# Where the negative maxima and the first of four sums stand on VectorE, and the order of the first sections, in a fused attention and GEGLU kernel

## The chip, the cores and the metric

The kernel runs on one core of a Trainium2 chip. Its metric is the device time of one execution in microseconds (us). Before the change the median of three runs is 2544.25 us (2543.74 to 2545.1).

A core has a TensorE (PE, matrix products; its weight loads, PEld, overlap the products), VectorE (DVE), ScalarE (ACT), GpSimd (POOL) and SyncE (SP, which here issues the transfers). The engines work side by side and wait for one another through semaphores.

## The reference

All is fp32: 2048 tokens of 576 numbers, 32 heads of 18, a hidden width of 4608.

```python
xn = layernorm(x)
qkv = xn @ wqkv                               # 576 x 1728
scores = einsum("bhqd,bhkd->bhqk", q, k) * 18 ** -0.5
s = (softmax(scores) @ v) @ wo
g = silu((gelu(xn @ w_gate) * (xn @ w_up)) @ w_down)   # 576 x 4608, twice; 4608 x 576
out = x + s * g
```

## The kernel before

**Arithmetic.** Products whose operands must be exact are made from fp32 numbers cut into a high and a low part (fp32r, `split`): high by high, high by low, low by high. Most matrix products use 64 rows of the array, so that two run side by side, one on the upper and one on the lower 64 rows ("row halves"). Only the products that add up attention's values (`acc`, L782) take all rows.

**Sections.** After the layer norm and the projections the feed-forward part is cut into 144 sections, 4 blocks of 512 tokens by 36 sections of 128 hidden units. A section's PE work begins with 27 pairs of matmuls (L413), pg for gate and pu for up. Then comes gelu on ACT and DVE: a square, DVE's first product L427, with pu the copy and product L438, the tanh L443, the last product L446 ("gelu's end"), and the cut of the hidden values (`finish`). Two sections together (G = 2) give the hidden values of one run of products with w_down.

**Sums with w_down.** `half_downs` (from L482) multiplies the hidden values with w_down. It is called one section later. Each sum is a bank py of 128 × 288, made of products on both row halves (L473); when the last one is in, `add_down` (L454) adds it into Y on DVE (L461). In most sections the run has eight sums, with banks taken in the order "mmsmfmss" and every second section; in sections 2 to 11 it has four ("smss"). The letters are the three groups of PSUM banks: "f" (two banks, shared with pg and pu), "m" (three, shared with the maxima and acc) and "s" (three, shared with the scores).

`half_downs` also calls what is left of gelu (`FF["rest"]`) from between its products: PE passes a mark, a tiny ACT copy waits on it, and tanh comes behind that copy. In the last run of a token block (`late = 2`) this happens one sum later than elsewhere, and L446 then follows the first sum added.

**Attention between the sections.** Sections 10 to 137 carry attention as specials spread between their gate and up pairs: a unit is 4 heads by 512 queries and takes 4 sections. A score pe (L747) is followed by its exponential on ACT (L748). The maximum over keys is needed one unit ahead: 40 places earlier a product pm (L709) is made and DVE reduces it (L712). When a unit's maxima are complete, `max_neg` (L719 to 728) forms the negative maxima on DVE: a reduction nm (L724), a copy to fp32r (L725), the subtraction that gives the low part (L726) and a transpose (L727), and sends them to DRAM (L728). `max_rows` then loads them as extra rows of the queries q. This happens in every fourth section: 12, 16, ... 132. There `max_neg` stands ahead of gelu on DVE. A reciprocal (L816) follows in the same section after the eight sums.

**The first sections.** Sections 0 to 9 hold no scores; `FIRST` says how many pairs of maxima for the first unit each holds. The first unit's `max_neg` stands in section 8. Ahead of section 0 SP issues the first keys KS and queries q; the first raw tile of w_down is loaded (`load_down`, L540) when section 1 is issued.

**Order.** PE's order is the program's. For the other engines a scheduler sets the order; `kept` and `keep_in_program_order` hold an instruction to the program's order, and `no_sync(a, b)` puts a behind b on their engine without a semaphore.

Of the kernel before, what the change touches and what calls it, by code (L numbers as in the profile page):

```python
# [10 lines left out]
AF = mybir.ActivationFunctionType  # L11
ALU = mybir.AluOpType
# [26 lines left out]
G = 2  # L39
NR = F // (G * P)  # L40
NF = NB * NR * G
FIRST = (0, 0, 4, 5, 5, 5, 5, 5, 5, 6)
ATT = range(len(FIRST), len(FIRST) + NU * NA)
MROW = 3 * DH
MH = 16
# [9 lines left out]
def f(ap):  # L55
    return ap.bitcast(F32)
# [13 lines left out]
def kernel(ctx: ExitStack, tc: tile.TileContext, x, wqkv, wo, w_gate, w_up, w_down, out):  # L70
# [86 lines left out]
    with tc.tile_pool(name="pro", bufs=1) as pro, tc.tile_pool(name="pps", bufs=1, space=PSUM) as pps:  # L157
# [189 lines left out]
        for b in range(NB):  # L347
# [41 lines left out]

    asked.clear()  # L390
    copied.clear()
    FF = {"w": ahead, "xd": XD, "down": [], "n": 0, "keep": None, "late": [],
          "Y": ffn.tile([P, TB // P, D], F32, name="Y")}
    mark = const.tile([P, 1], F32, name="mark")
    nc.vector.memset(mark, 0.0)
# [1 line left out]
    def kept(i):  # L397

        if FF["keep"]:
            tc.keep_in_program_order(i)  # L400
        return i
# [21 lines left out]
    def activate(pg, pu, early):  # L423

        t1 = ffn.tile([P, TB], F32, name="t1", bufs=2)
        kept(nc.scalar.activation(t1, pg, AF.Square))  # L426
        one = kept(nc.vector.scalar_tensor_tensor(t1, t1, 1.0 / GC, pg, op0=ALU.add, op1=ALU.mult))  # L427
        late = [m() for m in FF["late"]]
        FF["late"] = []
        for m in late:  # L430
            no_sync(m, one, "the activation's first product first")
        t2 = ffn.tile([P, TB], F32, name="t2", bufs=1) if early else None

        def times(behind=None, _=None):
            one = nc.scalar.activation(t2, pu, AF.Copy)
            if behind:
                no_sync(one, behind, "a mark first")
            two = nc.vector.tensor_tensor(t2, t2, pg, op=ALU.mult)  # L438
            for m in late:
                no_sync(two, m, "a maximum first")  # L440

        def rest(behind=None, evicted=None):
            tanh = kept(nc.scalar.activation(t1, t1, AF.Tanh, scale=GC * GS))  # L443
            if behind:
                no_sync(tanh, behind, "a mark first")
            one = kept(nc.vector.scalar_tensor_tensor(t1, t1, 1.0, t2 if early else pg, op0=ALU.add, op1=ALU.mult))  # L446
            if evicted:
                no_sync(one, evicted, "a finished sum first")
            if not early:
                kept(nc.vector.tensor_tensor(t1, t1, pu, op=ALU.mult))  # L450

        return t1, [times, rest] if early else [rest]

    def add_down(b, r, py, Y, j, c):  # L454
        yy = Y[:, j, 288 * c:288 * c + 288]
# [26 lines left out]
    def half_downs(b, r, hs, wd, Y, js, banks):  # L482

        m = len(DOWN)
        sums = [(j, c) for j in js for c in range(2)]
        low = len(sums) - 2
        pys, seen, evicted = {}, {}, None
        late = 2 if r == NR - 1 else 1  # L490

        def downs_of(a, ks):
            for k in ks:
                for i in range(m):
                    def step(k=k, i=i):
                        nonlocal evicted
                        j, c = sums[k]
                        fresh = k not in pys
                        if fresh:
                            pys[k] = bank(banks[k])  # L500
                        begun = a if k < low else 1 - a
                        one = down_product(pys[k], hs, wd, j, c, i, slice(HR * a, HR * a + HR), fresh,
                                           begun == 0 and i == m - 1)
                        if begun == 0 and i == 0 and k in seen:
                            after(one, seen[k])
                        if i == m - 1:
                            if begun == 0:
                                evicted = add_down(b, r, pys[k], Y, j, c)
                            elif a == 1 or len(sums) == 4:
                                seen[k] = behind(one)  # L510
                                if k in (0, late) and FF["rest"]:
                                    FF["rest"].pop(0)(seen[k], evicted if k == 2 else None)
                    yield step

        n = range(len(sums))
        rows = [*downs_of(0, n[low:]), *downs_of(0, n[:low])], [*downs_of(1, n)]
        for i, both in enumerate(zip(*rows, strict=True)):
            for half in both if i < low * m + m else both[::-1]:
                half()
# [19 lines left out]
    def load_down(r, raw):  # L539
        kept(nc.sync.dma_start(raw, w_down[r * G * P:(r + 1) * G * P, :].rearrange("(g p) n -> p g n", p=P)))  # L540
        return raw

    def section(specials=(), tag="f", raw_d=None, ahead=True):

        n = FF["n"]
        FF["n"] += 1
        b, r = divmod(n // G, NR)
        g = n % G
        pairs, pg, pu = gate_up(tag)
        if g == 0:  # L550
            FF["hs"] = []
        keep = kept
        if asked:
            xd_last = asked.pop()

            def keep(i):
                no_sync(i, xd_last, "transposed x first")
        nxt = None
        if n + 1 < NF:
            nxt = load_gu((n + 1) % (NR * G), keep) if ahead else FF.pop("next_gu")  # L560
        if nxt:
            for k in range(NG - 1 if ahead else 0):
                first = split_gu(nxt, k, kept)
                if k == 0 and n in ATT and n > ATT.start:
                    no_sync(first, FF["hl"], "hidden values first")
        if g == G - 1:
            FF["rawd"] = load_down(r, raw_d() if raw_d else raw_tile([P, G, D])) if ahead else FF.pop("next_d")
        for p in spread(pairs, specials):
            p()
        if nxt and ahead:  # L570
            split_gu(nxt, NG - 1, kept)
        FF["w"] = nxt
        if n + 1 < NF and (n + 1) % (NR * G) == 0:
            FF["xd"] = load_xd(b + 1, FF["key"])
        FF["act"], FF["rest"] = activate(pg, pu, n < ATT.stop)
        now = FF["down"] and FF["down"][0][-1] < FF["n"]
        if n < ATT.stop and not now:
            run_rest()
# [5 lines left out]
    def downs():  # L584
        while FF["down"] and (FF["down"][0][-1] < FF["n"] or FF["n"] == NF):
            down(*FF["down"].pop(0)[:-1])

    def finish(pool=ffn, cut=split, bufs=1):

# [66 lines left out]
    with tc.tile_pool(name="att", bufs=1, reuse_waits="tile") as att:  # L656
# [59 lines left out]
            else:  # L716
                reduce()

        def max_neg(u, keep=lambda i: i):  # L719

            nm = att.tile([P, MH], F32, name="nm", bufs=1)
            m2 = att.tile([P, 2 * MH], F32R, name="m2", bufs=1)
            m2t = att.tile([P, SQ], F32, name="m2t", bufs=1)
            keep(nc.vector.tensor_reduce(nm, MX[u].rearrange("p a t c -> p (a t) c"), axis=AX.X, op=ALU.max, negate=True))  # L724
            nc.vector.tensor_copy(m2[:, 0:MH], nm)  # L725
            nc.vector.tensor_tensor(m2[:, MH:2 * MH], nm, f(m2)[:, 0:MH], op=ALU.subtract)  # L726
            nc.vector.transpose(m2t, f(m2))  # L727
            nc.sync.dma_start(mT[u], m2t)  # L728

        def max_rows(u):  # L730

# [87 lines left out]
        def lead_raw():  # L819
            t = att.tile([P, QD, TB], F32, name="pT", bufs=8)  # L820
            return t.rearrange("p a t -> p (a t)")[:, 0:G * D].rearrange("p (g d) -> p g d", g=G)

        for r in range(2):
            load_k(0, rs=(r,))
            load_q(0, (r,))
# [4 lines left out]
        for n, m in enumerate(FIRST):  # L830
            none = [lambda: None]
            lead = [lambda s=s: lead_pair(s, s == slot + m - 1) for s in range(slot, slot + m)]
            section((1 + (n == 2)) * none * (m > 0) + lead, "s" if n == 1 else "f", lead_raw)
            if slot + m >= NS > slot:
                max_neg(0, tc.keep_in_program_order)
                max_rows(0)
            slot += m
            while n > 1 and chunk < KB and chunk * SLOTS <= slot + SLOTS:
                load_k(chunk, tc.keep_in_program_order)
                chunk += 1  # L840
            if n == 3:
                load_q(1)
            if n >= len(FIRST) - 2:
                load_v(n - len(FIRST) + 2)
            downs()
            run_rest()
            finish(cut=split_ap)
        for n in range(NU * NA):
            u, i = divmod(n, NA)
            s0 = n * SLOTS  # L850
# [10 lines left out]
            tasks(n, 0)  # L861
            um, im = divmod(s0 + LEAD + SLOTS, NS)
            if im == 0 and um <= NU:
                max_neg(um - 1)
                at(n + 1, 0, max_rows, um - 1)
            if i % 2:
                for kt in range((i - 1) * VC, (i + 1) * VC):
# [193 lines left out]
```

## Time and profile before

| | |
|---|---|
| median of 3 runs | 2544.25 us |
| the profiled execution's own time | 2543.24 us |
| its span on the core | 2541.4 us |
| granted TensorE clock | 1.0 |
| scores pe (L747) | 2048, 775.6 us of PE |
| exponentials (L748) | 2048, 1153.4 us of ACT |
| maxima reduced (L712) | 2048, 1250.2 us of DVE |
| sums added into Y (L461) | 544, 226.1 us of DVE |
| gate and up, high parts (L413) | 2592 each, 926 us of PE each |

A row of a timeline has the start, the duration, the engine, line and operation, the tile written and those read, their shapes and the count of alike instructions in a row; in brackets stands the time that the engine sat idle before it and what released it. A row of windows has the stretch, its length, the busy time of PE, PEld, DVE, ACT and POOL (with the count of instructions), the granted clock, the share of the DMA engines in use and the GB/s. Gate and up matmuls overlap, since they use different row halves, so busy times per line add up to more than the span.

### The profile page before, as it was taken

Reading aid. Unit: us, or ns where it says so; the run is one execution under the profiler, and the core shown is the slowest. Engines: PE = TensorE matmul, PEld = TensorE weight load, DVE = VectorE, ACT = ScalarE, POOL = GpSimd, SP = SyncE. Lnnn points to the kernel's source line nnn. Section 1 sums busy time; section 2 is a strip of 40 time slices with the busy share of each in tenths; the row PEclk is TensorE's granted clock in tenths of the full one; section 3 lists DMA queues with packets and bytes.
Section 4 is the critical chain, followed back from the end, with each engine's and each line's share of the span. In section 5 each row is a group of like instructions: output and inputs, shape, how many; then the busy total and the mean of one; then the engine's idle time right before and its main releaser. Section 6 shows DMA issues by size and latency. Waiting matters only on the chain.

```text
span 2541.4 us, 63721 instructions
## 1 busy us (share of the span) xinstructions
PE 2534.5 (100%) x24214; PEld 2022.0 (80%) x24214; DVE 1947.5 (77%) x3491; ACT 1563.5 (62%) x3098; POOL 1320.0 (52%) x1447
## 2 busy tenths in 40 slices
PE   9999999999999999999999999999999999999999
PEld 8889977777778877777777777777777777777698
DVE  5316978888888888888888888888888888887277
ACT  3223467666667766667666667666666666676622
POOL 2127644555565554445565554554446555455575
PEclk9999999999999999999999999999999999999999
DMA  8875444444464444444455444344446444443483
GB/s 267 266 242 151 110 107 104 110 103 110 108 155 114 109 103 110 113 113 111 111 129 142 111 109 108 105 104 112 108 112 157 111 110 109 107 109 97 116 238 109
DMA packets 398688, 325.54 MB, mean 128 GB/s; under 512 B 117408, under 2 KB 309184, under 8 KB 398384
## 3 DMA queue, kind: packets, MB, share of 16 engines
q1 hardware_dynamic: 398384, 321.47, 48.8%
q8 instruction: 193, 3.16, 0.5%
q14 instruction: 111, 0.91, 0.1%
HBM read 266.63 MB, written 54.70 MB: 126 GB/s over the span
## 4 chain that ended last, share of the span: by engine, by line
PE 98%; ACT 1%; DVE 0%; POOL 0%; issue 0%; POOLq 0%; ACTq 0%
PE pg L413 29%; PE py L473 18%; PE acc L782 18%; PE pm L709 9%; PE pe L747 9%; PE po L180 7%; PE pu L413 6%; PE po L921 2%; ACT pT L748 1%; PE pt L241 0%; PE po L232 0%; DVE t L446 0%; POOL dl L113 0%; POOL hl L113 0%; ACT t L426 0%
## 5 line engine op out<-in xcount | busy, mean ns | idle before, releaser
L748 ACT ACTIVATE pT<-pe 128x512 f32<-128x512 f32 x2048 | 1153.4, 598 | 364.6 <-PE pm L709 224.0
L712 DVE TENSOR_REDUCE mx<-pm 128x1 f32<-128x512 f32 x2048 | 1250.2, 682 | 148.2 <-PE pm L709 146.0
L413 PE MATMUL pu<-xd,wh 64*128 64x512 f32 x2592 | 925.9, 390 | 0.2 <-DVE t L438 0.2
L413 PE MATMUL pg<-xd,wh 64*128 64x512 f32 x2592 | 925.7, 390 | 0.0
L709 PE MATMUL pm<-KS,q 64*128 64x512 f32 x2048 | 779.2, 387 | 0.0
L747 PE MATMUL pe<-q,KS 64*128 64x512 f32 x2048 | 775.6, 387 | 0.9 <-DVE Y L461 0.9
L413 PEld LDWEIGHTS pg<-xd,wh 64*128 64x128 f32 x2592 | 476.9, 184 | 110.3 <-POOL wh L106 19.3
L413 PE MATMUL pg<-xd,wl 64*128 64x512 f32 x1296 | 501.3, 387 | 0.0
L413 PE MATMUL pu<-xd,wl 64*128 64x512 f32 x1296 | 501.3, 387 | 0.0
L413 PEld LDWEIGHTS pu<-xd,wh 64*128 64x128 f32 x2592 | 477.0, 184 | 1.1 <-DVE t L438 0.6
L782 PE MATMUL acc<-pT,VS 128*32 128x512 f32 x4096 | 452.8, 594 | 0.0
L108 POOL TENSOR_TENSOR wl<-raw,wh 128x384 fp32r<-128x384 f32 x432 | 433.4, 1016 | 14.0
L106 POOL TENSOR_SCALAR hh<-t 128x512 fp32r<-128x512 f32 x128 | 79.1, 618 | 663.3 <-DVE t L446 648.6
L709 PEld LDWEIGHTS pm<-KS,q 64*128 64x128 f32 x2048 | 374.9, 184 | 25.4 <-DVE mx L712 1.3
L747 PEld LDWEIGHTS pe<-q,KS 64*128 64x128 f32 x2048 | 370.5, 184 | 22.6 <-DVE Y L461 1.9
L473 PE MATMUL py<-dh,hh 64*128 64x288 f32 (+1 forms) x2240 | 366.0, 293 | 0.2
L473 PE MATMUL py<-dl,hh 64*128 64x288 f32 (+1 forms) x2240 | 365.3, 292 | 0.1
L473 PE MATMUL py<-dh,hl 64*128 64x288 f32 (+1 forms) x2240 | 364.5, 292 | 0.0
L782 PEld LDWEIGHTS acc<-pT,VS 128*32 128x32 f32 x4096 | 127.3, 110 | 289.9 <-issue 278.4
L106 POOL TENSOR_SCALAR wh<-raw 128x384 fp32r<-128x384 f32 x432 | 217.2, 514 | 137.6 <-PE pu L413 82.7
L461 DVE TENSOR_TENSOR Y<-py,Y 128x288 f32<-128x288 f32 x544 | 226.1, 452 | 53.5 <-PE py L473 46.3
L413 PEld LDWEIGHTS pg<-xd,wl 64*128 64x128 f32 x1296 | 238.6, 184 | 30.3
(120 smaller groups left out, 3135.3 us busy)
## 6 DMA issues: line engine op xcount, KB each, us to landing
KS<-qk SPq DMA_DIRECT2D x1536, 36.0 KB
raw<-in_B_w_gate_dram SPq DMA_DIRECT2D x144, 288.0 KB
raw<-in_B_w_up_dram SPq DMA_DIRECT2D x144, 288.0 KB
raw<-in_B_w_down_dram SPq DMA_DIRECT2D x67, 576.0 KB
VS<-vs SPq DMA_DIRECT2D x128, 152.0 KB
qk<-t SPq DMA_DIRECT2D x72, 256.0 KB
q<-qk SPq DMA_DIRECT2D x384, 36.0 KB
xx<-in_A_x_dram SPq DMA_DIRECT2D x32, 288.0 KB
```

Of the source, the lines that this page charges most:

```text
L106: first = nc.gpsimd.tensor_scalar(hi, raw, 1.0, 1.0, op0=ALU.mult, op1=ALU.mult)
L108: low_part[:] = [keep(nc.gpsimd.tensor_tensor(lo, raw, f(hi), op=ALU.subtract))]
L180: nc.tensor.matmul(o, st, m, start=(i == 0), stop=(i == len(terms) - 1))
L413: nc.tensor.matmul(o, w[1 + wp][k][rr, c, :], xd[xp][k][rr, c, :], start=(i == 0), stop=(i == len(terms) - 1))
L461: one = kept(nc.vector.tensor_tensor(yy, py, yy, op=ALU.add))
L473: return nc.tensor.matmul(py, hs[g][a][rr, j * P:(j + 1) * P], wd[w][rr, g, 288 * c:288 * c + 288], start=start, stop=stop)
L709: nc.tensor.matmul(pm, QS[u, r][rr, t * P:(t + 1) * P], KS[(u * NA + c) % KB][r][rr, :], start=True, stop=True)
L712: return nc.vector.tensor_reduce(MX[u][:, 2 * r + a, t, c:c + 1], pm, axis=AX.X, op=ALU.max)
L747: nc.tensor.matmul(pe, KS[(u * NA + c) % KB][r][rr, t * P:(t + 1) * P], QS[u, r][rr, :], start=True, stop=True)
L748: nc.scalar.activation(PT[u, kt][:, 2 * r + a, :], pe, AF.Exp, scale=SCALE)
L782: nc.tensor.matmul(ACC[u][32 * a:32 * a + 32, :], VS[(u * NA + c) % VB][:, v:v + 32], pt[:, a, :], start=first, stop=last, skip_group_chec ...
L921: nc.tensor.matmul(po, parts_of(b, j)[x_][:, k, :], OW[w][c][k], start=(i == 0), stop=(i == len(OUT) - 1))
```

## The change

Five edits.

1. `max_neg` no longer issues its four steps but returns them as a list (`FF["between"]`). In a run of eight sums, nm is issued after the third finished sum, copy and subtraction after the fourth, and each holds the next sum behind itself; what is left (the transpose with its transfer) is issued when the run has been issued. The scheduler's order on DVE is then, in 27 of the 31 places: gelu's end, three sums, nm, a sum, copy, subtraction, transpose, reciprocal, four sums. In sections 36, 72 and 108 the first sum stands ahead of gelu's end as before, and in section 12 there is no reciprocal. The first unit's four steps stand in section 8, behind the fourth maximum of that section.
2. `rest` becomes `tanh` and `rest`. In runs of four sums, gelu's end (L446) is issued behind the first finished sum and ahead of the second.
3. `FIRST` gives every section from 2 to 9 five pairs of maxima, and one empty place ahead of them in all: section 2 gets a fifth pair, section 9 loses its sixth.
4. The first raw tile of w_down is loaded ahead of the first keys and queries.
5. The first unit's `max_rows` is issued at the end of its section.

PE's instructions are the same in number; their order differs only in where maxima stand in sections 2 to 9. ACT's order is the same. POOL's and SP's differ in a few places of each unit (the transfer of the negative maxima is issued later in its section).

```diff
-FIRST = (0, 0, 4, 5, 5, 5, 5, 5, 5, 6)
+FIRST = (0, 0) + (5,) * 8
...
-        def rest(behind=None, evicted=None):
-            tanh = kept(nc.scalar.activation(t1, t1, AF.Tanh, scale=GC * GS))
+        def tanh(behind=None, _=None):
+            one = kept(nc.scalar.activation(t1, t1, AF.Tanh, scale=GC * GS))
             if behind:
-                no_sync(tanh, behind, "a mark first")
+                no_sync(one, behind, "a mark first")
+
+        def rest(_=None, evicted=None):
             one = kept(nc.vector.scalar_tensor_tensor(t1, t1, 1.0, t2 if early else pg, op0=ALU.add, op1=ALU.mult))
             if evicted:
                 no_sync(one, evicted, "a finished sum first")
             if not early:
                 kept(nc.vector.tensor_tensor(t1, t1, pu, op=ALU.mult))
-
-        return t1, [times, rest] if early else [rest]
+            return one
+
+        return t1, [times, tanh, rest] if early else [tanh, rest]
...
                                 evicted = add_down(b, r, pys[k], Y, j, c)
+                                if ahead:
+                                    no_sync(evicted, ahead, "between two finished sums")
+                                    ahead = None
+                                done += 1
+                                if done == 1 and len(sums) == 4 and len(FF["rest"]) == 1:
+                                    ahead = FF["rest"].pop(0)(None, evicted)
+                                for _ in range({3: 1, 4: 2}.get(done, 0) if len(sums) > 4 and FF["between"] else 0):
+                                    ahead = FF["between"].pop(0)(evicted)
                             elif a == 1 or len(sums) == 4:
                                 seen[k] = behind(one)
                                 if k in (0, late) and FF["rest"]:
-                                    FF["rest"].pop(0)(seen[k], evicted if k == 2 else None)
+                                    FF["rest"].pop(0)(seen[k])
+                                if k == late and FF["rest"] and len(sums) > 4:
+                                    FF["rest"].pop(0)(None, evicted if k == 2 else None)
...
         if g == G - 1:
-            FF["rawd"] = load_down(r, raw_d() if raw_d else raw_tile([P, G, D])) if ahead else FF.pop("next_d")
+            FF["rawd"] = FF.pop("first_d") if n < G else load_down(r, raw_d() if raw_d else raw_tile([P, G, D])) if ahead else \
+                FF.pop("next_d")
...
     def downs():
         while FF["down"] and (FF["down"][0][-1] < FF["n"] or FF["n"] == NF):
             down(*FF["down"].pop(0)[:-1])
+        while FF["between"]:
+            FF["between"].pop(0)()
...
-        def max_neg(u, keep=lambda i: i):
+        def max_neg(u):
...
-            keep(nc.vector.tensor_reduce(nm, MX[u].rearrange("p a t c -> p (a t) c"), axis=AX.X, op=ALU.max, negate=True))
-            nc.vector.tensor_copy(m2[:, 0:MH], nm)
-            nc.vector.tensor_tensor(m2[:, MH:2 * MH], nm, f(m2)[:, 0:MH], op=ALU.subtract)
-            nc.vector.transpose(m2t, f(m2))
-            nc.sync.dma_start(mT[u], m2t)
+
+            def step(what):
+                def go(behind=None):
+                    one = what()
+                    if behind:
+                        no_sync(one, behind, "a finished sum first")
+                    return one
+                return go
+
+            def square():
+                one = nc.vector.transpose(m2t, f(m2))
+                nc.sync.dma_start(mT[u], m2t)
+                return one
+
+            return [step(what) for what in (
+                lambda: nc.vector.tensor_reduce(nm, MX[u].rearrange("p a t c -> p (a t) c"), axis=AX.X, op=ALU.max, negate=True),
+                lambda: nc.vector.tensor_copy(m2[:, 0:MH], nm),
+                lambda: nc.vector.tensor_tensor(m2[:, MH:2 * MH], nm, f(m2)[:, 0:MH], op=ALU.subtract),
+                square)]
...
+        FF["first_d"] = load_down(0, lead_raw())
         for r in range(2):
             load_k(0, rs=(r,))
             load_q(0, (r,))
...
-            section((1 + (n == 2)) * none * (m > 0) + lead, "s" if n == 1 else "f", lead_raw)
+            section((m > 0) * none + lead, "s" if n == 1 else "f", lead_raw)
             if slot + m >= NS > slot:
-                max_neg(0, tc.keep_in_program_order)
-                max_rows(0)
+                FF["between"] = max_neg(0)
...
+            full = len(FF["between"]) > 0
             downs()
             run_rest()
             finish(cut=split_ap)
+            if full:
+                max_rows(0)
...
             if im == 0 and um <= NU:
-                max_neg(um - 1)
+                FF["between"] = max_neg(um - 1)
                 at(n + 1, 0, max_rows, um - 1)
```

More of the change, by code (lines that the diff above doesn't have):

```diff
@@ L391 @@
     copied.clear()
-    FF = {"w": ahead, "xd": XD, "down": [], "n": 0, "keep": None, "late": [],
+    FF = {"w": ahead, "xd": XD, "down": [], "n": 0, "keep": None, "late": [], "between": [],
           "Y": ffn.tile([P, TB // P, D], F32, name="Y")}
@@ L490, in half_downs @@
         late = 2 if r == NR - 1 else 1
+        done, ahead = 0, None
         def downs_of(a, ks):
@@ L495, in step @@
                     def step(k=k, i=i):
-                        nonlocal evicted
+                        nonlocal evicted, done, ahead
                         j, c = sums[k]
```

## The prediction

> **What bounds the kernel now.** I read the page first (busy times, chain of waits), then the windows of single sections, then the timelines of VectorE (DVE) and PE around the places that the change touches.
>
> ```profile
> span 2541.4 us, 63721 instructions
> PE 2534.5 (100%) x24214; PEld 2022.0 (80%) x24214; DVE 1947.5 (77%) x3491; ACT 1563.5 (62%) x3098; POOL 1320.0 (52%) x1447
> PE 98%; ACT 1%; DVE 0%; POOL 0%; issue 0%; POOLq 0%; ACTq 0%
> ```
>
> PE sets the end: 98% of the chain is its own work. The diff moves PE instructions but adds none, so a gain can only come from PE's short stalls and a loss from new ones. They are too small for the page and show in the lengths of sections, counted from one section's first gate matmul to the next one's.
>
> ```profile
> 397.21:413.50 16.28, 16.28 (x186) 14.56 (x184) 14.61 (x29) 12.25 (x26) 5.19 (x8) 1.00 0.33 90
> 413.50:430.48 16.98, 16.98 (x155) 11.61 (x152) 12.68 (x23) 10.74 (x19) 9.83 (x11) 1.00 0.44 104
> 430.48:446.72 16.25, 16.25 (x186) 14.53 (x184) 14.76 (x26) 11.70 (x25) 8.24 (x12) 1.00 0.43 124
> 446.72:463.61 16.89, 16.89 (x154) 11.15 (x151) 12.58 (x22) 10.65 (x19) 10.98 (x11) 1.00 0.56 118
> sum 764.89, PE 764.89 PEld 601.82 DVE 627.68 ACT 528.74 POOL 352.41; mean PE 33.26 PEld 26.17 DVE 27.29 ACT 22.99 POOL 15.32
> sum 762.14, PE 762.14 PEld 588.61 DVE 629.74 ACT 514.35 POOL 443.73; mean PE 33.14 PEld 25.59 DVE 27.38 ACT 22.36 POOL 19.29
> 729.17:762.30 33.13, 33.13 (x336) 25.67 (x333) 27.28 (x51) 22.89 (x45) 21.94 (x25) 1.00 0.67 158
> ```
>
> The columns are microseconds, then the busy time of PE, PEld, DVE, ACT and POOL. Negative maxima are formed in sections 12, 16, 20, ... 132 (31 places) and, for the first unit, in section 8. Section 16 is 397.21 to 413.50. The first sum is over 23 pairs of sections that begin with such a place, the second over the 23 pairs that follow each: 764.89 − 762.14 = 2.75, or 0.120 us for each place. The pair at 729.17 (section 36) holds such a place and has 33.13, no excess: there, as in 72 and 108, a finished sum already stands ahead of gelu's end. So 28 places × 0.120 = 3.35 us can be removed.
>
> Where the 0.12 is from, in DVE's timeline of section 16:
>
> ```profile
> 407.97 0.22 DVE L724 TENSOR_REDUCE nm<-mx 128x16 f32<-128x64 f32 x1
> 408.23 0.17 DVE L725 CAST m<-nm 128x16 fp32r<-128x16 f32 x1
> 408.44 0.17 DVE L726 TENSOR_TENSOR m<-nm,m 128x16 fp32r<-128x16 f32 x1
> 408.53 0.68 DVE L427 SCALAR_TENSOR_TENSOR t<-t,pg 128x512 f32<-128x512 f32 x1
> 409.13 0.20 DVE L727 STREAM_TRANSPOSE m2t<-m 128x32 f32<-128x32 f32 x1
> 409.25 0.65 DVE L438 TENSOR_TENSOR t<-t,pg 128x512 f32<-128x512 f32 x1
> 410.01 0.69 DVE L446 SCALAR_TENSOR_TENSOR t<-t,t 128x512 f32<-128x512 f32 x1
> 410.62 1.18 DVE L461 TENSOR_TENSOR Y<-py,Y 128x288 f32<-128x288 f32 x3
> 414.56 0.24 DVE L816 RECIPROCAL sums<-sums 128x16 f32<-128x16 f32 x1
> 414.72 0.63 DVE L712 TENSOR_REDUCE mx<-pm 128x1 f32<-128x512 f32 x1
> ```
>
> The chain stands ahead of gelu (L427 starts 0.56 after L724), so the run of finished sums starts late, and PE's upper row half waits for the first bank to be read. PE shows it at the head of the next section, where the half with pu lags:
>
> ```profile
> 413.50 0.39 PE L413 MATMUL pg<-xd,wh 64*128 64x512 f32 x1
> 413.62 0.39 PE L413 MATMUL pu<-xd,wh 64*128 64x512 f32 x1
> 446.72 0.39 PE L413 MATMUL pg<-xd,wh 64*128 64x512 f32 x1
> 446.72 0.40 PE L413 MATMUL pu<-xd,wh 64*128 64x512 f32 x1
> ```
>
> With a place pu is 0.12 behind pg (413.62 − 413.50); without one 0.00. The lag is paid when the odd section ends in values that need all rows: 16.98 − 16.89 and 16.28 − 16.25 make the 0.12.
>
> **The change part by part.**
>
> *Negative maxima between sums.* The order after is: three sums, nm, the fourth sum, copy, subtraction, transpose, then the reciprocal, then sums five to eight. Removed: −3.35. What it costs is read off a section without a place (18):
>
> ```profile
> 443.57 1.41 DVE L461 TENSOR_TENSOR Y<-py,Y 128x288 f32<-128x288 f32 x3
> 445.32 0.46 DVE L461 TENSOR_TENSOR Y<-py,Y 128x288 f32<-128x288 f32 x1 [0.34 <-PE py L473]
> 446.12 1.62 DVE L461 TENSOR_TENSOR Y<-py,Y 128x288 f32<-128x288 f32 x4 [0.34 <-PE py L473]
> ```
>
> The first three sums end at 444.98 and the fourth starts at 445.32, when PE is done with its bank: nm (0.22) fits the 0.34 and costs nothing. From the fourth to the fifth PE leaves 446.12 − 445.32 = 0.80. In it now stand: the fourth sum, 0.37 until the next may start (four sums take 1.62, so (1.62 − 0.46)/3 = 0.39, three 1.18, so 0.36); copy to subtraction 0.21 (408.23 to 408.44); as much again to the transpose; transpose to the next 0.12 (409.13 to 409.25); reciprocal to the next 0.16 (414.56 to 414.72). Together 1.08 with roundings, 0.28 late: the fifth sum starts at 446.40 and ends at 446.86 instead of 446.58. Its bank is one of the two of the tag "f", and the next section's pu takes it, due at 446.72. With 0.05 from the end of a sum to PE's start, pu starts at 446.91: 0.19 late, 0.14 beyond the lag that sections without a place carry to their end anyhow (0.04, my estimate from the 0.12 that costs 0.09 at the odd section). By the same settling as above that is 0.14 × 31 = +4.3. Bounds: 0, where pu's half finds its time again, and 0.28 × 31 = 8.7, where the whole lateness goes through. I take the middle value, since the row at 413.62 shows lag and price to be about equal (0.12 each). The order holds in the three places that had no excess and in section 12, so 31 and not 28.
>
> A page of the Trainium skill, "VectorE: DVE Perf Modes", section "The DRAIN you can't avoid", has it that the next operation does not start before the pipe of the one in front is empty. By that, the pieces would follow end to start (a rival below). The trace differs: sums of 0.46 start 0.37 apart.
>
> *Early sections.* Sections 8 to 10, and where the first unit's chain stands:
>
> ```profile
> 272.95:283.53 10.57, 10.57 (x116) 10.42 (x113) 10.05 (x21) 3.99 (x9) 8.41 (x8) 1.00 0.45 114
> 283.53:295.49 11.97, 11.72 (x118) 9.18 (x116) 11.59 (x22) 2.94 (x8) 5.82 (x7) 1.00 0.17 41
> 276.56 4.40 DVE L712 TENSOR_REDUCE mx<-pm 128x1 f32<-128x512 f32 x7
> 282.33 0.21 DVE L724 TENSOR_REDUCE nm<-mx 128x16 f32<-128x64 f32 x1
> 283.46 0.65 DVE L438 TENSOR_TENSOR t<-t,pg 128x512 f32<-128x512 f32 x1
> 284.17 0.49 PE L413 MATMUL pu<-xd,wh 64*128 64x512 f32 x1 [0.25 <-DVE t L438]
> ```
>
> Before, the chain (282.33 to 283.46, 1.13 us) holds L438, and pu of section 9 waits for it until 284.17, 0.64 behind pg. Section 9 also has six pairs of maxima. It comes down from 11.97 to the 10.6 of section 8: −1.37. In section 8 the chain moves behind the fourth maximum. Maxima follow each other by (4.40 − 0.68)/6 = 0.62, so the chain would run from 277.77 to 278.90 and the fifth maximum would end at 279.58; the bank for the eighth is due at about 278.80: +0.83 (0.5 if the copy takes the 0.17 of section 16 here). Net −0.54.
>
> Section 2 gets a fifth pair (+0.23, the rate of gate/up pairs) and its first maxima fall behind L446 of section 1:
>
> ```profile
> 209.09:219.90 10.80, 10.67 (x112) 9.52 (x110) 8.68 (x14) 6.16 (x14) 8.00 (x8) 1.00 0.74 182
> 211.31 0.69 DVE L446 SCALAR_TENSOR_TENSOR t<-t,t 128x512 f32<-128x512 f32 x1
> 214.00 2.67 POOL L113 TENSOR_TENSOR dl<-pT,dh 128x1152 fp32r<-128x1152 f32 x1
> 208.21 0.41 SPq L540 DMA_DIRECT2D pT<-in_B_w_down_dram  x1
> 212.04 0.39 PE L709 MATMUL pm<-KS,q 64*128 64x512 f32 x2
> ```
>
> L446 holds DVE to 212.00, so the fourth maximum waits some 0.35; against that the wait for dl, ready at 216.67 and needed earlier by the 0.4 that PE now comes later, goes. Net +0.2 (0 to +0.6).
>
> *w_down first.* Its load (208.21) moves ahead of the first keys. Nothing before dl is freed by it: POOL reaches dl at 214.00 behind its other split. Cost 0: q's last piece, issued just ahead of 208.21, goes out 0.41 later, at about 208.6, and its first use is at 212.04, 3.4 us after that; gone that cover, it is a rival.
>
> *Runs of four sums.* One sum goes ahead of gelu's end in sections 2 to 11:
>
> ```profile
> 296.21 0.50 PE L747 MATMUL pe<-q,KS 64*128 64x512 f32 x1 [0.26 <-DVE Y L461]
> PE pe L747 <- DVE Y L461: 0.9, 3, 0.3
> ```
>
> Three waits of the first scores for the first sum, 0.9 us in all, are at the heads of sections 10, 11 and 12 (0.5 to 0.6 of lag each). The sum earlier frees the scores, but then the maxima behind L446 bind by 0.3: gain 0.27 + 0.18 + 0.25 = −0.7 (0 to −1.6).
>
> Sum: −3.35 + 4.3 − 0.54 + 0.2 − 0.7 + 0 = −0.1. The profiled execution took 2543.24 (span 2541.4 and 1.8 around it), 1.01 below the median 2544.25. So 2543.24 − 0.1 + 1.01 = 2544.2.
>
> **The rivals.** First: the fifth sum is late but pu is not, because the chain overlaps more than these rows say (for: L427 starts 0.09 after L726; against: copy, subtraction and transpose depend on one another, and stand 0.21 apart). Then +4.3 is 0: −4.4, 2539.9, and with the full −1.6 in sections 10 to 12, 2539.0.
>
> Second, on the slower side: the late fifth bank holds both halves, since PE issues in order and pg's next pair stands behind pu. It decides once pu is later than a pair's 0.23. Price 0.28 × 31 = 8.7 in place of 4.3: +4.3, 2548.6; without the −0.7 of the early sections 2549.3. Against it: 0.19 is under 0.23.
>
> Third: the keys queue behind w_down's 576 KB (2 × 128 rows of 576 numbers) and come after 212.04. At the 182 GB/s of section 2's window, 576 KB take 3.2 us, which with the 0.41 fills 3.6 of the 3.8 us between 208.21 and 212.04; a piece that flies 1.2 us (my guess, no row has it) is then 1.0 late: 2545.2. Against: it is then issued ahead of all the keys, and should be through by q's last piece.
>
> Fourth: nothing of the chain overlaps: 0.46 + 0.17 + 0.17 + 0.21 + 0.24 = 1.25 in the 0.80, so 0.45 late, pu 0.35 late, both halves held: 31 × 0.35 = 10.9 for 4.3, sum +6.5, 2550.7. This is what the Trainium skill's drain rule would make of it. Against: the overlaps above.
>
> **How the numbers follow.** Forecast 0.55, first rival 0.22, second 0.14, third 0.05, fourth 0.04. 0.2% (5.1 us, about what a measurement of this kernel can tell from no change) is passed at 2539.2 and 2549.3. Faster: half of the first rival, 0.12. Slower: the fourth and about a third of the second, 0.09. Same 0.79. The range goes from the first rival with its full early gain, 2538.9, to the second, 2549.0; beyond lie the fourth and the second's edge. The forecast alone: 2542 to 2546.5.
>
> **What would show it.** Pairs of sections with a place should come to 33.13 + 0.14, as before; pu at the head of the next section should stand 0.15 to 0.2 behind pg, waiting for a sum; the fifth sum should start 1.08 after the fourth. Section 9 should take 10.6, section 8 about 11.4, section 2 about 11.0, and the three waits of scores for sums be gone. The forecast is wrong if pairs with a place reach 33.13 (first rival) or pass 33.35 (second, fourth), or if section 2 waits for keys.

## The result and the profile after

The changed kernel takes 2556.41 us (median of six runs, 2554.89 to 2558.06) against 2543.66 (six runs, 2542.88 to 2545.1) before. The ratio is 1.005, 95% interval 1.0037 to 1.0063: 12.75 us slower, outside the range and on the side that had a chance of 0.09. The profiled execution after, the fastest of its six runs, has a span 11.4 us longer than the one before (2552.8 against 2541.4), so the two traces show where most of that time went.

From the profile's page after, and from the waits of PE's weight loads in the whole span one row (total, times, longest, in us):

```profile
span 2552.8 us, 63830 instructions
PE 98%; DVE 1%; ACT 1%; issue 0%; DMA 0%; SPq 0%; ACTq 0%; DVEq 0%
```

```profile
PEld pu L413 <- DVE Y L464: 9.3, 28, 1.0
```

PE is still the bound. What is new is this wait: in 28 sections, each behind one that forms negative maxima, the weights of pu wait for a finished sum. Before, pu had no such row. Lines have moved: the sums are L464, the four steps L756, L757, L758 and L751, the reciprocal L847, gelu's end L448.

The same four sections as in the prediction (16 to 19), and section 36, where a new token block begins, with 37, in the windows after:

```profile
396.27:412.52 16.25, 16.25 (x186) 14.53 (x183) 14.57 (x29) 12.26 (x26) 5.48 (x9) 1.00 0.32 90
412.52:429.81 17.29, 17.29 (x155) 11.44 (x152) 12.98 (x23) 10.43 (x19) 11.71 (x12) 1.00 0.32 77
429.81:446.05 16.24, 16.24 (x186) 14.52 (x184) 14.77 (x26) 11.71 (x25) 6.21 (x10) 1.00 0.49 134
446.05:462.91 16.86, 16.86 (x155) 9.88 (x152) 12.58 (x22) 10.64 (x19) 10.97 (x11) 1.00 0.61 133
...
729.70:745.95 16.25, 16.25 (x187) 14.53 (x183) 14.60 (x26) 12.26 (x26) 12.68 (x13) 1.00 0.86 174
745.95:763.77 17.82, 17.39 (x156) 10.72 (x152) 13.47 (x26) 10.44 (x19) 10.16 (x11) 1.00 0.32 109
```

The section with a place lost its 0.03 (16.28 to 16.25), but the one behind it went from 16.98 to 17.29, and behind section 36 from 16.89 to 17.82. From the starts of all sections in both traces, the 28 places that had an excess are 0.317 slower each (median; 9.4 together; a place is counted as the pair of sections that begins with it), sections 36, 72 and 108 by 0.93, 1.19 and 0.94 (3.1 together), and sections 0 to 11 are 0.5 faster.

DVE in section 16 after, from the first sum on, and POOL at the same time:

```profile
409.37 1.41 DVE L464 TENSOR_TENSOR Y<-py,Y 128x288 f32<-128x288 f32 x3
410.69 0.21 DVE L756 TENSOR_REDUCE nm<-mx 128x16 f32<-128x64 f32 x1
411.12 0.46 DVE L464 TENSOR_TENSOR Y<-py,Y 128x288 f32<-128x288 f32 x1 [0.22 <-PE py L476]
411.50 0.16 DVE L757 CAST m<-nm 128x16 fp32r<-128x16 f32 x1
411.69 0.36 DVE L758 TENSOR_TENSOR m<-nm,m 128x16 fp32r<-128x16 f32 x1
412.09 0.21 DVE L751 STREAM_TRANSPOSE m2t<-m 128x32 f32<-128x32 f32 x1
412.23 0.21 DVE L847 RECIPROCAL sums<-sums 128x16 f32<-128x16 f32 x1
412.35 1.49 DVE L464 TENSOR_TENSOR Y<-py,Y 128x288 f32<-128x288 f32 x4
```

```profile
410.25 1.30 POOL L108 TENSOR_TENSOR hl<-t,hh 128x512 fp32r<-128x512 f32 x1
411.51 1.00 POOL L106 TENSOR_SCALAR wh<-raw 128x384 fp32r<-128x384 f32 x2
```

The order is the announced one, and nm is free. But the subtraction takes 0.36 where it took 0.17 before, and it ends (412.05) when the first of POOL's two cuts of weights does (it begins at 411.51 and takes 0.52). In section 36 it is the copy:

```profile
744.92 0.89 DVE L757 CAST m<-nm 128x16 fp32r<-128x16 f32 x1
```

```profile
744.49 1.28 POOL L108 TENSOR_TENSOR hl<-t,hh 128x512 fp32r<-128x512 f32 x1
```

The copy ends at 745.81, 0.04 behind POOL's cut of the hidden values (745.77). The fifth sum follows the fourth by 1.23 in section 16 (411.12 to 412.35), not by 1.08; 0.80 is what PE leaves in a section without a place.

### The profile page after: what moved, and what is told of

Read it like the earlier page. It is cut to its first block, busy times and chain, and to the rows that moved or that the text cites. A ratio compares the mean times of both kernels' runs of the same rounds, so it can differ in the third digit from the quotient of the medians.

```text
span 2552.8 us, 63830 instructions
## 1 busy us (share of the span) xinstructions
PE 2542.9 (100%) x24214; PEld 1996.6 (78%) x24214; DVE 1958.7 (77%) x3491; ACT 1556.0 (61%) x3098; POOL 1323.2 (52%) x1447
## 4 chain that ended last, share of the span: by engine, by line
PE 98%; DVE 1%; ACT 1%; issue 0%; DMA 0%; SPq 0%; ACTq 0%; DVEq 0%
PE pg L413 27%; PE acc L813 18%; PE py L476 17%; PE pm L726 9%; PE pe L778 9%; PE pu L413 8%; PE po L180 7%; PE po L955 2%; ACT pT L779 1%; PE pt L241 0%; DVE Y L464 0%; DVE m L757 0%; DMA xx<-in_A_x_dram 0%; DVE mx L729 0%; DVE m L758 0%
## 5 line engine op out<-in xcount | busy, mean ns | idle before, releaser
L476 PE MATMUL py<-dh,hh 64*128 64x288 f32 (+1 forms) x2240 | 348.3, 292 | 0.2
L476 PE MATMUL py<-dh,hl 64*128 64x288 f32 (+1 forms) x2240 | 347.7, 292 | 0.0
L476 PE MATMUL py<-dl,hh 64*128 64x288 f32 (+1 forms) x2240 | 347.6, 292 | 0.0
L464 DVE TENSOR_TENSOR Y<-py,Y 128x288 f32<-128x288 f32 x544 | 224.8, 449 | 41.8 <-PE py L476 33.8
```

The costliest lines, as they stand in the source:

```text
L464: one = kept(nc.vector.tensor_tensor(yy, py, yy, op=ALU.add))
L476: return nc.tensor.matmul(py, hs[g][a][rr, j * P:(j + 1) * P], wd[w][rr, g, 288 * c:288 * c + 288], start=start, stop=stop)
```

## The experiments

Each kernel was timed against the kernel before on the same chip. Places are counted as above; "for each place" is the median of the 28, against before, from the profiled executions.

| kernel | us | before beside it | ratio, 95% interval | for each place |
|---|---|---|---|---|
| the changed kernel | 2556.41 | 2543.66 | 1.0037 to 1.0063 | +0.317 |
| undo_neg | 2542.1 | 2543.36 | 0.9987 to 1.0004 | +0.003 |
| one_input | 2547.8 | 2543.36 | 1.0011 to 1.0029 | +0.116 |
| two_behind | 2549.67 | 2543.36 | 1.0014 to 1.0036 | −0.003 |
| three_ahead | 2547.3 | 2543.36 | 1.0006 to 1.0024 | −0.037 |
| pool_waits | 2550.29 | 2543.66 | 1.0017 to 1.0037 | +0.133 |
| one_copy | 2554.28 | 2543.66 | 1.0027 to 1.0059 | +0.306 |
| trans_third | 2540.2 | 2543.66 | 0.9976 to 0.9994 | −0.070 |
| sub_first_sum | 2539.21 | 2543.66 | 0.9973 to 0.9991 | −0.120 |
| f_third | 2577.75 | 2543.47 | 1.0122 to 1.015 | +0.767 |
| w_down_later | 2539.91 | 2543.47 | 0.9977 to 0.9996 | −0.130 |
| first_unit_behind | 2538.49 | 2543.47 | 0.9973 to 0.999 | −0.130 |

**undo_neg: the negative maxima ahead of gelu again.**

```diff
-                FF["between"] = max_neg(um - 1)
+                for go in max_neg(um - 1):
+                    go()
```

> The changed kernel with the chain of negative maxima ahead of gelu again in the 31 places of the attention sections; all other edits stay. Theory A (copy and subtraction, now placed while POOL cuts hidden values and weights, are held by POOL's instruction: subtraction 0.36 us for 0.17, copy 0.9 in sections 36, 72, 108): the other edits are worth what their sections show, about -1.0, so 2542.7 us. Rival B (five DVE steps between two sums are too many whatever POOL does): the same, 2542.7. Rival C (w_down first, or the order of sums in runs of four, costs the time): near 2556.

2542.1, as A and B expected. The whole loss belongs to the first edit, in its 31 places; the others together are worth −1.26 by the medians, with an interval that still takes in 1. Rival C falls.

**one_input: the steps without a copy and without two SBUF inputs.**

```diff
-                lambda: nc.vector.tensor_copy(m2[:, 0:MH], nm),
-                lambda: nc.vector.tensor_tensor(m2[:, MH:2 * MH], nm, f(m2)[:, 0:MH], op=ALU.subtract),
+                lambda: nc.vector.tensor_reduce(m2[:, 0:MH], nm.rearrange("p (c o) -> p c o", o=1), axis=AX.X, op=ALU.max),
+                lambda: nc.vector.tensor_reduce(m2[:, MH:2 * MH], f(m2)[:, 0:MH].rearrange("p (c o) -> p c o", o=1), axis=AX.X, op=ALU.max),
```

> The changed kernel with copy and subtraction replaced by two reductions over an axis of one, which read one SBUF tensor each; the number and order of the steps stay. The low part of the negative maxima is left out (the high part stands there twice). Theory A: no step is held by POOL any more; they take some 0.2 each, the fifth sum follows the fourth by 1.05 to 1.1 instead of 1.23, pu lags by 0.1 to 0.2, sections 36, 72 and 108 behave like the rest; about 2547 us (2545 to 2549). Rival B: nothing changes, 2556.

2547.8. DVE's timeline of section 16 of this kernel:

```profile
412.18 0.46 DVE L464 TENSOR_TENSOR Y<-py,Y 128x288 f32<-128x288 f32 x1 [0.22 <-PE py L476]
412.56 0.16 DVE L757 TENSOR_REDUCE m<-nm 128x16 fp32r<-128x16 f32 x1
412.75 0.17 DVE L758 TENSOR_REDUCE m<-m 128x16 fp32r<-128x16 f32 x1
412.95 0.21 DVE L751 STREAM_TRANSPOSE m2t<-m 128x32 f32<-128x32 f32 x1
413.09 0.21 DVE L847 RECIPROCAL sums<-sums 128x16 f32<-128x16 f32 x1
413.22 1.12 DVE L464 TENSOR_TENSOR Y<-py,Y 128x288 f32<-128x288 f32 x3
```

Same number of steps in the same places, POOL at work beside them as before, and now 1.04 from the fourth sum to the fifth. Rival B expected no change and falls. A was right for ordinary places and wrong for the three others: sections 36, 72 and 108 with those behind them stay 1.0, 0.3 and 0.8 above before. There another step is late. Gelu's end takes 1.12, 0.90 and 1.47 instead of 0.69; in section 108:

```profile
1941.50 1.47 DVE L448 SCALAR_TENSOR_TENSOR t<-t,t 128x512 f32<-128x512 f32 x1 [0.40 <-ACT t L443]
```

```profile
1941.40 1.01 POOL L108 TENSOR_TENSOR wl<-raw,wh 128x384 fp32r<-128x384 f32 x1
```

It begins beside one of POOL's cuts of weights and goes on for 0.56 after this cut has ended. Like the subtraction it reads two tensors in SBUF.

**pool_waits: POOL waits, DVE untouched.**

```diff
+                one = FF["turned"] = nc.vector.transpose(m2t, f(m2))
...
                     no_sync(first, FF["hl"], "hidden values first")
+                    if FF.get("turned"):
+                        after(first, FF.pop("turned"))
```

> The changed kernel, DVE untouched; POOL's first cut of the next section's weights waits for the transpose of the negative maxima, so that it no longer runs beside the subtraction. Theory A (POOL holds the read path): subtraction 0.17 instead of 0.36 in ordinary places, the fifth sum follows the fourth by 1.05 instead of 1.23, pu lags by about 0.1 instead of 0.28; sections 36, 72, 108 stay, since their copy is held by the cut of hidden values, which doesn't wait: 2550 us (2548 to 2552). Rival B (the chain is too long by itself, POOL's overlap is a coincidence): 2556.4 or, since weights come later, more.

2550.29. In section 16:

```profile
410.96 0.46 DVE L464 TENSOR_TENSOR Y<-py,Y 128x288 f32<-128x288 f32 x1 [0.21 <-PE py L476]
411.33 0.16 DVE L759 CAST m<-nm 128x16 fp32r<-128x16 f32 x1
411.53 0.17 DVE L760 TENSOR_TENSOR m<-nm,m 128x16 fp32r<-128x16 f32 x1
...
412.00 1.49 DVE L464 TENSOR_TENSOR Y<-py,Y 128x288 f32<-128x288 f32 x4
```

```profile
412.10 0.99 POOL L106 TENSOR_SCALAR wh<-raw 128x384 fp32r<-128x384 f32 x2 [0.72 <-DVE sums L849]
```

The very subtraction that took 0.36 takes 0.17 when POOL's cut comes behind it; the fifth sum follows the fourth by 1.04. Rival B falls. With this and one_input, POOL's hold is shown from both sides: of +0.317 a place it makes 0.18 to 0.20. Sections 36, 72 and 108 don't just stay, they are 1.5, 1.3 and 0.9 above before: their copy is held as in the changed kernel, and in 36 and 72 gelu's end takes 1.30 and 1.09 too.

**one_copy: the copy alone replaced** (the first of one_input's two lines).

> The changed kernel with the copy alone replaced by a reduction over an axis of one; the subtraction, with its two SBUF tensors, stays. Theory A in the form that an operation with two SBUF inputs is held as much as a copy: ordinary places stay (subtraction 0.36, lag 0.28), and in sections 36, 72 and 108 the subtraction takes over the wait (0.7 instead of the copy's 0.9) with the same lag: 2556. If only the copy can be held for long, the three sections lose their extra 0.6 each: 2554.

2554.28. The trace shows the first form, the subtraction taking over the wait, in sections 36 and 108; in 36:

```profile
744.75 0.16 DVE L757 TENSOR_REDUCE m<-nm 128x16 fp32r<-128x16 f32 x1
744.95 0.69 DVE L758 TENSOR_TENSOR m<-nm,m 128x16 fp32r<-128x16 f32 x1
```

POOL's cut of the hidden values runs from 744.32 to 745.60 there, and the subtraction ends at 745.64. So a subtraction with two SBUF inputs is held like a copy. In section 72 the subtraction takes 0.18, but gelu's end takes 1.04. The time is nearer to the second form's 2554. In the traces the three places lose 2.4 instead of 3.1, which is less than half of the difference, and the runs of the two kernels overlap (2553.01 to 2555.99 here): it is an answer on the mechanism; the 2 us are not.

**two_behind and three_ahead: transpose and reciprocal behind the eighth sum.** In the first kernel copy and subtraction stay behind the fourth sum, in the second the first three steps go ahead of gelu.

```diff
         while FF["between"]:
-            FF["between"].pop(0)()
+            FF["between"].pop(0)(FF["last"])
...
+            if FF["last"]:
+                no_sync(one, FF["last"], "the last sum first")
```

> The changed kernel with transpose and reciprocal held behind the eighth sum; copy and subtraction stay behind the fourth. Theory A: the subtraction is still held (0.36), the fifth sum follows the fourth by 0.97, pu lags under 0.1 in ordinary places, which costs next to nothing, but in sections 36, 72 and 108 the copy still takes 0.9 and pu lags by some 0.55: 2541.5 us (2540 to 2544). Rival B: two of five steps gone, so two fifths of the 13.7 gone: 2551.

> Reduction, copy and subtraction ahead of gelu, where POOL stands idle, transpose and reciprocal behind the eighth sum; all other edits stay. Gelu's end is then some 0.2 later than in sections without a place, not 0.32. Theory A: copy and subtraction take 0.17 each; if the first 0.2 of lateness is free, as the lag of 0.12 for 0.32 suggests, the pairs of sections reach 33.13 and the time is 2539.4 us; if lag goes in proportion, 0.075 for each of 28 places stays: 2541.5. Rival B has the same here; it differs from A in the lengths of copy and subtraction alone.

2549.67 and 2547.3: both times missed. The ordinary places did come down (the lag is 0.00 and 0.06), but sections 36, 72 and 108 with their successors rose by 1.9, 1.7 and 2.0 and by 1.1, 2.3 and 0.9. In the first, pu of sections 37 and 109 waits 1.1 and 1.3 for the fifth sum, behind a held copy (0.97 and 0.96) and a held gelu's end (1.32 and 1.52). In the second, and in section 72 of the first, PE waits for the next block's x, which POOL copies; of the second:

```profile
PE pu L413 <- POOL xd L146: 1.2, 2, 0.9
```

These two waits are in section 72; in 36 and 108 only the weight loads of pu wait for x (0.48 and 0.46). Nothing of the kind stood in PE's waits before. Later transfers on SP in the sections ahead are the likely cause, but that was only argued; the next two kernels go round it. two_behind also shows that lag 0 is not all: its place is worth −0.003, not −0.12. Its section 17 loses the difference at its head, where pu starts with pg but the next product of pu comes 0.58 behind it instead of 0.48; what made this step longer is not shown.

**trans_third and sub_first_sum: the transpose behind the third sum, the last run of a block as before the change.** The second kernel also puts the subtraction behind the first sum.

```diff
                 FF["between"] = max_neg(um - 1)
+                for _ in range(4 if (FF["n"] - 1) % (NR * G) == 0 else 3):
+                    FF["between"].pop(0)()
...
-                                for _ in range({3: 1, 4: 2}.get(done, 0) if len(sums) > 4 and FF["between"] else 0):
+                                for _ in range({3: 1}.get(done, 0) if len(sums) > 4 and FF["between"] else 0):
```

(sub_first_sum has 2 for 3 and `{1: 1, 3: 1}`; both hold the reciprocal behind the eighth sum.)

> Reduction, copy and subtraction ahead of gelu, the transpose alone behind the third sum, where DVE waits for PE anyway; in sections 36, 72 and 108 the whole chain ahead of gelu as before the change. All other edits stay. Theory: the transfer of the negative maxima goes out early enough that SP's queue holds nothing up; a lag of 0.06 stays, so 28 places gain some 0.06 each beside undo_neg: 2540.5 us, against 2539.4 if the lag of 0.06 costs nothing.

> Reduction and copy ahead of gelu, the subtraction behind the first sum, the transpose behind the third; sections 36, 72 and 108 as before the change. All other edits stay. Gelu's end is then 0.04 late and the lag 0; the subtraction, beside POOL's cut of hidden values, takes up to 0.5, which the pause ahead of the fourth sum (0.64 of issue time) hides: 28 x 0.12 less than undo_neg, 2538.8 us. If the second and third sums' lateness reaches the fourth, 0.1 to 0.2 a place is given back: 2542 to 2544.

2540.2 and 2539.21; both are faster than before with an interval below 1. Section 16 of sub_first_sum, DVE, then sections 16 and 17 in the windows:

```profile
409.91 0.45 DVE L464 TENSOR_TENSOR Y<-py,Y 128x288 f32<-128x288 f32 x1
410.28 0.45 DVE L759 TENSOR_TENSOR m<-nm,m 128x16 fp32r<-128x16 f32 x1
410.65 0.81 DVE L464 TENSOR_TENSOR Y<-py,Y 128x288 f32<-128x288 f32 x2
411.38 0.19 DVE L752 STREAM_TRANSPOSE m2t<-m 128x32 f32<-128x32 f32 x1
411.67 0.46 DVE L464 TENSOR_TENSOR Y<-py,Y 128x288 f32<-128x288 f32 x1
412.46 1.62 DVE L464 TENSOR_TENSOR Y<-py,Y 128x288 f32<-128x288 f32 x4 [0.33 <-PE py L476]
```

```profile
396.82:413.06 16.24, 16.24 (x186) 14.52 (x184) 14.80 (x29) 12.26 (x26) 5.47 (x9) 1.00 0.33 89
413.06:429.95 16.89, 16.89 (x154) 11.14 (x151) 12.66 (x23) 10.65 (x19) 11.75 (x12) 1.00 0.28 65
```

The subtraction is held by POOL here too (0.45, until the first of POOL's cuts of the hidden values ends), but ahead of a pause, and the fifth sum waits for PE again. The pair is 33.13, the length of a pair without a place.

**f_third: another bank for the fifth sum.**

```diff
-                half_downs(b, r, hs, wd, Y, range(TB // P), "mmsmfmss")
+                half_downs(b, r, hs, wd, Y, range(TB // P), "mmfmsmss")
```

> The changed kernel with two banks of the run of eight exchanged: the third sum stands in the bank of pu, the fifth in one of the scores' (mmfmsmss for mmsmfmss). DVE's chain and POOL's hold stay as they are. Theory A2 (the price is made at pu: its weight load waits for the fifth sum's bank, and the loads of the scores, the maxima and the next pg, which need nothing, stand behind it in order): pu doesn't wait, lag 0, and with the 0.44 of lateness still there the places cost next to nothing: 2541 us (2540 to 2544). Rival D (the price is the lateness itself, since the sums six to eight and the first maxima come 0.44 later too): 2549 or more.

2577.75, far off A2's 2541; D's "2549 or more" takes it in, but not for D's reason, since sections without a place grow as well (16.43 and 16.98 for 18 and 19). Two rows of the weight loads' waits are new against the changed kernel:

```profile
PEld pe L778 <- DVE Y L464: 12.2, 30, 0.9
PEld py L476 <- ACT t L435: 10.4, 63, 0.3
```

The second row is the exchange's own price: the third sum now takes pu's bank, and its products wait until ACT has copied pu out. The first is the late sum's: the score takes pu's part. At the head of section 21 of this kernel PE has

```profile
481.30 0.50 PE L778 MATMUL pe<-q,KS 64*128 64x512 f32 x1
```

with pe 0.56 behind pg (480.74), where it stood 0.23 behind in section 19 before. A late sum is paid for by what takes its bank next. The time doesn't tell A2 from D.

**w_down_later: w_down's first load back behind the keys, on sub_first_sum.** The line `FF["first_d"] = load_down(0, lead_raw())` and its use are taken out.

> The version with the subtraction behind the first sum (sub_first_sum), with w_down's first load back behind the first keys and queries. Theory: w_down first is worth nothing either way, 2539.2 us as with it (2538.7 to 2539.7). Rival: it holds or frees section 2, and the time moves by more than 0.5.

2539.91 (2538.62 to 2541.83) against 2539.21 (2538.78 to 2539.99) with it. The medians are 0.7 apart, but the runs overlap, and section 2 is 0.18 above before in the one and 0.15 in the other. That w_down first is worth something is not shown.

**first_unit_behind: the first unit's steps behind the fourth sum of section 8, on sub_first_sum.**

```diff
-                                FF["last"] = evicted if len(sums) > 4 else None
+                                FF["last"] = evicted
...
-            FF["between"].pop(0)()
+            FF["between"].pop(0)(FF["last"])
```

> The same version with the first unit's four steps behind the fourth sum of section 8 instead of between its maxima. Section 8 then loses the 1.1 that it gained, section 9 starts its maxima some 0.9 late, of which its three banks hide a part: 2538.5 us (2538 to 2539). Rival: section 9 gives all of it back, 2539.2.

2538.49, as forecast, and the lowest median here, though its runs (2537.83 to 2540.82) overlap with those of sub_first_sum. In the traces sections 8 and 9 together are 0.92 under before, against 0.29 in sub_first_sum.

## Why the prediction was wrong, by its steps

**Removed, −3.35: right.** sub_first_sum leaves only the reduction and the copy ahead of gelu and adds no new wait, and its 28 places are 3.6 faster than before.

**The cost between the sums, +4.3: wrong, and the whole miss.** Measured from pairs of sections without a place, it is about 15.8 (9.4 + 3.35 in the 28 places, 3.1 in the three others). It failed at three points. (A slip besides: 0.19 less the 0.04 carried anyhow is 0.15, not 0.14, 0.3 us in the sum.)

First, the chain's length. The prediction had "copy to subtraction 0.21 (408.23 to 408.44); as much again to the transpose". The transpose followed the subtraction by 0.40 (411.69 to 412.09). With POOL out of the way the sum of the overlaps was right: from the fourth to the fifth sum 1.08 forecast, 1.04 in one_input and pool_waits. The 0.21 was read where POOL stands idle: in that stretch of section 16 before, POOL's timeline has no instruction. Between the sums POOL cuts hidden values and weights. The trace of before had a warning in section 8:

```profile
282.58 0.50 DVE L725 CAST m<-nm 128x16 fp32r<-128x16 f32 x1
```

```profile
282.04 1.01 POOL L108 TENSOR_TENSOR wl<-raw,wh 128x384 fp32r<-128x384 f32 x1
```

The copy ended at 283.08, 0.03 behind POOL. The prediction used this 0.50 as an odd value beside 0.17 and didn't ask what held it. The Trainium skill, page "SBUF — State Buffer", section "SBUF: two separate sides", says that DVE and GpSimd share a pair of SBUF ports as an exclusive lock: of a GpSimd operation and a DVE operation that is in a two-port mode, or that has two SBUF inputs beside a GpSimd operation that reads SBUF, the one that starts first keeps the ports to its end and the other waits. By that the subtraction can be held, and the copy if it runs in such a mode, for as long as what POOL has begun; the traces agree (0.36, 0.89 and 0.69, each ending within 0.04 of POOL's end). The reductions that stand in their places take 0.16 and 0.17 beside the same cuts, and the transpose takes no more than 0.21 in any of the thirteen traces.

Second, the price of the lag. "0.14 × 31" took a lag of pu at its own length, from the row at 413.62. PE and its weight loads at the head of section 17 after:

```profile
412.52 0.39 PE L413 MATMUL pg<-xd,wh 64*128 64x512 f32 x1
412.81 0.50 PE L413 MATMUL pu<-xd,wh 64*128 64x512 f32 x1
412.81 0.50 PE L778 MATMUL pe<-q,KS 64*128 64x512 f32 x1
413.15 0.39 PE L726 MATMUL pm<-KS,q 64*128 64x512 f32 x1
```

```profile
412.80 0.18 PEld L413 LDWEIGHTS pu<-xd,wh 64*128 64x128 f32 x1 [0.23 <-DVE Y L464]
412.81 0.18 PEld L778 LDWEIGHTS pe<-q,KS 64*128 64x128 f32 x1
412.99 0.18 PEld L726 LDWEIGHTS pm<-KS,q 64*128 64x128 f32 x1
```

pu's weights wait for the bank, and the loads of the score and the maximum, which need nothing from it, come behind. pu and pe take 0.50 instead of 0.39, and pm starts 0.63 after pg, against 0.25 in section 19 before (446.97 − 446.72). So a lag of 0.28 ends as 0.40 in the section's length (17.29 − 16.89). In one_input a lag of 0.09 costs 0.24 a place above pairs without one (0.116 + 0.120). The row at 413.62 was of another kind: there the whole row half already ran 0.13 late in the sums, and pu's load waited for nothing:

```profile
413.49 0.18 PEld L413 LDWEIGHTS pu<-xd,wh 64*128 64x128 f32 x1
```

The price is made at the head. Over the 27 ordinary places behind section 12 the fourth product of pu stands 0.44 later than in sections without a place (median), and the section is 0.45 longer; in one_input both are 0.24. The late sums six to eight and the late maxima behind the head add next to nothing, which is A2's account and not D's. The second rival's held half, pg, shows in section 17 after (its second product comes 0.63 behind the first, 412.52 to 413.15), with a lag past its 0.23; but one_input pays more than its lag without reaching 0.23. The reading rests on these rows; f_third was to test it by the time and did not.

Third, the three places of the last runs were counted like the others, at 0.14. They lost 0.93 to 1.19. In the changed kernel the copy there meets a cut of the hidden values that has just begun and takes 0.88 to 0.98. But that is not all of it: without this wait one_input still lost 0.3 to 1.0 there, because gelu's end was held in its turn. Behind the first sum, POOL's cuts can hold either step.

Together, for each of the 28 places: forecast −0.12 + 0.14 = +0.02; measured +0.317, of which 0.18 to 0.20 goes when POOL doesn't hold the chain; the rest is the price of the lag. The bound of 8.7 for this cost (0.28 × 31) was no bound, since the 0.28 left POOL out and a lag can cost more than its length.

**Early sections, −1.04 in all: right in sign, too large in size.** Section 9 is at 10.64 (forecast 10.6). Section 8 rose by 1.13 to 11.70, not by 0.83, so the two gave −0.2 and not −0.54. Section 2 rose by 0.16 (forecast 0.2). Sections 10 and 11 gave −0.38 (forecast −0.45), and the three waits of scores for sums are gone, as said. In undo_neg's trace, where the attention places are as before, sections 0 to 12 together are 0.8 faster; its −1.26 by the medians has an interval of some ±2 around it.

**w_down first, 0:** not contradicted.

**The rivals.** The first falls: pu was late. The third, keys late, didn't occur; its 1.2 us of flight was a guess, but the small transfers of the negative maxima (mT) do land from about 1.25 us after their issue in the trace of before. The fourth's 2550.7 was nearest, with the right kind of step (the chain longer than its overlaps allow) for a wrong reason: sums still start 0.37 apart, and the length came from POOL.

## What to carry to other kernels

A duration taken from a trace holds for the neighbours it was measured beside: before a step is moved, read what GpSimd does at the new place, above all for a copy or an operation with two SBUF inputs. A short operation can stand where its being late does no harm, ahead of a pause, but not ahead of the one sum whose bank the matrix engine takes next. And where the same step shows two durations in one trace, the odd one is a question to settle before the prediction, not a spread.

## What was not expected of the hardware

A 128 × 16 copy took from 0.16 to 0.98 us in the changed kernel by what GpSimd was doing (0.98 in section 72). In the thirteen traces, each of the 270 copies and subtractions of the chain that took over 0.2 us ended within 0.034 us behind a GpSimd operation. Gelu's end, with two SBUF inputs, took 0.69 where GpSimd was idle and up to 1.99 beside it (w_down_later, section 71), while the sums, with one of their inputs in PSUM, never took more than 0.46. A matmul whose weights waited for a semaphore took 0.50 us instead of 0.39 in section 17, and a place with a lag of 0.09 cost 0.24.
